# Staging later chunks' k and q in DRAM and loading them by blocks in four transfers

## The chip, the cores and the metric

The kernel runs on one core of a Trainium2 chip. The metric is device time in microseconds (us) from the start to the end of one execution, lower is better; a time given for a kernel is the median of its timed runs. Besides the timed runs there is one profiled execution, from which every duration in this text comes.

## What is computed

An mLSTM cell is followed by a two-layer network with GELU. Shapes: 4 batches (B), 8 heads (H), 768 steps (S), 40 values per head (D); the network takes 3072 tokens of 320 values through 2048 hidden ones and back.

```python
for t in range(S):
    m_new = np.maximum(f_gate[:, :, t] + m, i_gate[:, :, t])
    f_stab = np.exp(f_gate[:, :, t] + m - m_new)
    i_stab = np.exp(i_gate[:, :, t] - m_new)
    C = f_stab * C + i_stab * einsum('bhd,bhe->bhde', vt, kt)
    n = f_stab * n + i_stab * kt
    h_tilde = einsum('bhde,bhe->bhd', C, qt)
    denom = maximum(abs(einsum('bhd,bhd->bh', n, qt)), 1.0)
    y[:, :, t] = sigmoid(o_gate[:, :, t]) * h_tilde / denom
x = y as (tokens, 320)
out = gelu(x @ w_in) @ w_out
```

## The kernel before

**Chunks.** The 768 steps are cut into 6 chunks (c = 0 to 5) of 128 steps. Within a chunk the recurrence is written as matrix products: scores of k against q (`ps`), a weight matrix `W` of exponentials, values (`ph`), what the state of earlier chunks gives (`pf`), and an update of the state. One chunk of all four batches makes 512 tokens (`x`), which then go through the network: `up` (w_in, three products per weight piece, in which x stands as `x_hi`, `x_lo` and `x_all`, and GELU into the tile `g`) and `down` (w_out, in seven half-size products with sums of parts, line L895).

**Order.** The program is traced with a manual schedule: each engine's instructions stand in the order in which they are written. Two strings of words, FRONT and DOWN, are the order by hand. FRONT (the first 129 us) does the gates, the conversion of the weights, chunks 0 and 1 of the cell and chunk 0 of the network. Then, for c = 1 to 5, `up` of chunk c is played, and after it DOWN, which weaves the 14 down products of chunk c (word F) with the cell steps of chunk c+1. The words of DOWN that matter here, by batch number: L3 load batch 3's k and q by blocks (`load_last`), B3 load its row of maxima (`last_M`), K and Q turn k and q (`turn_k`, `turn_q`), C read the state, h update it, V values, M mask, W weights, Y finish, X turn y, R `split_x`, j load batch 0 of the chunk after (`load_next`). K and Q of batches 0 and 1 are done inside `up` (its `turns`).

**Blocks.** For chunks from 2 on, k and q are not transposed by TensorE. They are loaded as 32x32 blocks that VectorE's transpose then turns (L458). `load_blocks` (L153) does this for one batch: for k and q, for the first 32 and the last 8 of the 40 values, and for each of four groups of 32 steps, one transfer from the input: 16 transfers. Batches 0 to 2 go to the tile `blocks`; batch 3 goes into a part of the previous chunk's hidden tile `g` (`load_last`, L443), after GpSimd has zeroed two strips of it (L447, two memsets). The row of maxima of batch 3 also goes into a part of `g` (L177, 512 KB, copied to all partitions), that of the other batches into a tile `W` (L180, 512 KB).

**One queue.** All transfers are issued by SyncE (SP), in order; a transfer whose semaphores are not there yet holds up all behind it. The transfers use eight completion semaphores in turn, so that the n-th waits for the (n-8)-th to have landed. In DOWN the SP order is: batch 3's 16 block transfers, its maxima, then for batches as they are used up k and v (L148, L150) and `W` (L180) for three batches ahead, then 16 block transfers for batch 0 of the next chunk, then o_gate and the outputs.

**Buffers.** `x_lo` and `x_all` are tiles of their own, made once in `products_begin` (L695); `split_x` (L675) writes them for one batch at a time, and the matmuls of `up` (L820, L831) read them.

Of the kernel before, what the change touches and what calls it, by code (L numbers as in the profile page):

```python
# [9 lines left out]
F32 = mybir.dt.float32  # L10
F32R = mybir.dt.float32r
# [5 lines left out]
P = 128  # L17
# [22 lines left out]
def kernel(  # L40
# [16 lines left out]
    nc = tc.nc  # L57

    B, H, S, D = q.shape
    L = P  # L60
    NCH = S // L
# [7 lines left out]
    TG = B * L  # L69
    R = P // 2  # L70
    NX = 2
# [12 lines left out]
    dram = ctx.enter_context(tc.tile_pool(name="dram", bufs=1, space=bass.MemoryType.DRAM))  # L84
# [36 lines left out]
    beyond = gates.tile([P, L], BF16, name="beyond")  # L121
    f_sb = gates.tile([BH, NCH, L], F32, name="f_sb")
    i_sb = gates.tile([BH, NCH, L], F32, name="i_sb")
    M_d = dram.tile([NCH - 1, BH, L], F32, name="M_d")
    swapped_d = [dram.tile([P, n, BH], F32, name=f"swapped{n}") for n in (NCH - 2, NCH - 3)]

# [12 lines left out]
    def load(n, first=0, end=4):  # L139
# [4 lines left out]
        for src, dst in ((q, qb), (k, kb), (v, vb), (o_gate, None))[first:end]:  # L144
            if dst and swapped(c, b):
                x, to = src[b, :, c * L:(c + 1) * L, :].rearrange("h p d -> p h d"), dst[turn_of(n)][:, :, 0:D]
                for i in range(2):
# [2 lines left out]
            nc.sync.dma_start(out=dst[turn_of(n)][:, :, 0:D] if dst else out_of(n),  # L150
                              in_=src[b, :, c * L:(c + 1) * L, :].rearrange("h p d -> p h d"))

    def load_blocks(n, to):  # L153

        c, b = divmod(n, B)
        for i, src in enumerate((k, q)):
            for d, w in ((0, 32), (32, D - 32)):
                for g in range(4):
                    t = c * L + 32 * g
                    nc.sync.dma_start(out=to[64 * i + d:64 * i + d + 32, :, 32 * g:32 * g + w],  # L160
                                      in_=src[b, :, t:t + 32, d:d + w].rearrange("h t d -> t h d"))
# [116 lines left out]
    def decays_last(g0, g1):  # L278
        g = slice(g0, g1)
        pd = ps_tr.tile([P, g1 - g0, BH], F32, name="pd", tag="tr")  # L280
        nc.tensor.matmul(pd.rearrange("p c n -> p (c n)"), last, gT[:, g].rearrange("p c n -> p (c n)"),
                         start=True, stop=True)
        by_half = pd.rearrange("p c (n two) -> p c n two", two=2)
        for hip in range(2):
            nc.vector.tensor_copy(out=dec[halves[hip], g], in_=by_half[halves[hip], :, :, hip])
# [109 lines left out]
    class Cell:  # L395
# [46 lines left out]

        def load_last(self, b):  # L443

            self.by_block = self.before.t[:, 0:HF, 0:P]
            for r in (32, 96):
                nc.gpsimd.memset(self.by_block[r:r + 32], 0.0)  # L447
            load_blocks(self.c * B + b, self.by_block)
# [14 lines left out]
        def turn_q(self, b):  # L463
            self.turn_half(b, 1)
            if b < B - 2:
                load_blocks(self.c * B + b + 1, by_block)
            if self.c < NCH - 1 and b < B - 1:
                self.weigh_values(b)
# [205 lines left out]

        def split_x(self, b):  # L675
            px, t = self.px.pop(b), slice(b * L, (b + 1) * L)
            hi = parts["x"][:, :, t]
            nc.vector.scalar_tensor_tensor(out=parts["x_lo"][:, :, t], in0=px, scalar=-1.0 / BASE, in1=hi, op0=OP.mult, op1=OP.add)
            nc.vector.tensor_tensor(out=parts["x_all"][:, :, t], in0=px, in1=hi, op=OP.subtract)


    HF, HT, HD = NF // 2, TG // 2, DM // 2
# [9 lines left out]
    w_sums, parts, fars, w_hi, w_lo, w_mid = [], {}, [], [], [], {}  # L692
    T = {1: lambda j: w_sums[0][:, j, :], 2: lambda j: w_sums[1][:, j, :], 3: Bm[0][1]}

    def products_begin():  # L695

        gate_ctx.close()
        pool = ctx.enter_context(tc.tile_pool(name="parts", bufs=1))
        w_sums.extend(pool.tile([P, HF, HD], F32, name=f"w_sums{n}") for n in range(2))
        for name in ("x_lo", "x_all"):  # L700
            parts[name] = pool.tile([P, NX + 1, TG], F32R, name=name)
        fars.extend([pool])

    def split_weight():
        i = len(w_lo)
        if i in (0, 3, 5, 8):
            two = shared([P, NX, 2, WP // 2], F32R, "w_in_hi")
            w_hi.extend([two[:, 0], two[:, 1]])
        elif i == 2:
            two = shared([P, 2, 2, WP // 2], F32R, "w_rest_hi")  # L710
            w_hi.append(two[:, 0])
            rest_two.append(two[:, 1])
        elif i == 7:
            w_hi.append(rest_two[0])
        w = w_all[i]
        nc.scalar.activation(out=w_hi[i], in_=w, func=AF.Copy, scale=PART * 2.0 ** -12)
        w_lo.append(w_f(F32R, "w_in_lo"))
        nc.vector.scalar_tensor_tensor(out=w_lo[i], in0=w_hi[i], scalar=-BASE * 2.0 ** 12, in1=w, op0=OP.mult, op1=OP.add)
# [3 lines left out]
    def join_weight(i):  # L722
        w_mid[i] = raw.tile([P, 2, WP // 2], F32R, name="w_in_mid", tag="pow") if i % 5 in (1, 4) else w_f(F32R, "w_mid")
        nc.vector.tensor_tensor(out=w_mid[i], in0=w_hi[i], in1=w_lo[i], op=OP.add)  # L724
# [22 lines left out]
    def hidden_sums(g, f0, f1):  # L747

        (a11, a21), (_, a22) = [[g.t[:, HF * e + f0:HF * e + f1, HT * h:HT * (h + 1)] for h in range(2)]
                                for e in range(2)]  # L750
        s1, s2 = [t[f0 // (HF // 2)][:, f0 % (HF // 2):f0 % (HF // 2) + f1 - f0, :] for t in (g.s1, g.s2)]
        nc.vector.tensor_tensor(out=s1, in0=a21, in1=a22, op=OP.add)  # L752
        nc.vector.tensor_tensor(out=s2, in0=s1, in1=a11, op=OP.subtract)
        nc.vector.tensor_tensor(out=a21, in0=a11, in1=a21, op=OP.subtract)
# [44 lines left out]
    def up(g, sums_too, turns):  # L799

        def split_to(i):
            while len(w_lo) <= i:
                split_weight()

        def pair(f, ahead):

            at = [f // 2 * 5 + f % 2 * 3 + x for x in range(NX)]
            split_to(at[1])
            for i in at:
                if i not in w_mid:  # L810
                    join_weight(i)
            pus = [[pool.tile([P, TG], F32, name="pu", tag=tag) for e in range(2)]
                   for pool, tag in (((ps_h, "h"), (ps_mm, "a")), ((ps_tr, "tr"), (ps_mm, "b")))[f % 2]]
            ahead()
            mid = [w_mid.pop(i) for i in at]
            for n, (w, x) in enumerate((([w_hi[i] for i in at], parts["x"]), ([w_lo[i] for i in at], parts["x_lo"]), (mid, parts["x_all"]))):
                for i in range(2):
                    for e in range(2):
                        for k in range(NX):
                            nc.tensor.matmul(pus[i][e], w[k][:, e, i * P:(i + 1) * P], x[:, k, :],  # L820
                                             start=(n == 0 and k == 0), stop=False, skip_group_check=True)
            return pus

        def rest(u, banks, order):
            mid = w_mid.pop(5 * u + 2)
            for i in order:
                pu = banks[i]
                for n, (w, x) in enumerate(((w_hi[5 * u + 2], parts["x"]), (w_lo[5 * u + 2], parts["x_lo"]), (mid, parts["x_all"]))):
                    for e in range(2):
                        r = halves[e]  # L830
                        nc.tensor.matmul(pu[e], w[r, i // 2, i % 2 * P:(i % 2 + 1) * P], x[r, NX, :], start=False,  # L831
                                         stop=(n == 2), skip_group_check=True)

        def out(i, e, pu):
            nc.scalar.activation(out=g.t[:, HF * e + i, :], in_=pu[e], func=AF.Gelu, scale=4097.0)  # L835

        b0 = pair(0, lambda: split_to(4))
        b1 = pair(1, lambda: join_weight(2))
        for step in turns[:1]:
            step()  # L840
        rest(0, b0 + b1, (0, 1, 2, 3))
        split_to(6)
        join_weight(5)
        join_weight(6)
        for i, pu in enumerate(b0 + b1):
            for e in range(2):
                out(i, e, pu)
        for step in sums_too[:5]:
            step()
        b2 = pair(2, lambda: split_to(9))  # L850
        hidden_sums(g, 0, 2)
        b3 = pair(3, lambda: (hidden_sums(g, 2, 4), join_weight(7)))
        for step in turns[1:] + sums_too[5:]:
            step()
        rest(1, b2 + b3, (2, 3, 0, 1))
        for i, e in ((2, 0), (2, 1), (3, 0), (0, 0), (1, 0), (3, 1), (0, 1), (1, 1)):
            out(4 + i, e, (b2 + b3)[i])
        hidden_sums(g, HF - 2, HF)
        hidden_sums(g, HF - 4, HF - 2)
# [100 lines left out]
    def cell_steps(c, letters, before=None):  # L960
# [11 lines left out]
                 d=lambda: decays_last(0, 1), q=lambda: decays_last(1, NCH - 1), r=halves_out, p=halves_back,  # L972
# [5 lines left out]
    for c in range(1, NCH):  # L978
        g, later, steps = Hidden(True), [], {}
# [38 lines left out]
```

## Time and profile before

| what | value |
|---|---|
| timed runs | 480.09 us median of 3 (479.88 to 480.18) |
| profiled execution | 482.25 us; its span, from the first to the last instruction, 480.3 us |
| busy share of the span | TensorE matmul 98%, weight load 85%, VectorE 73%, ScalarE 46%, GpSimd 16% |
| data queue q1 | 170,368 packets, 43.73 MB, 46.1% of the time of 16 DMA engines |
| instruction queue q8 | 42 packets of 16 KB |
| issues by SP, of these block transfers of L160 | 442, 256 |
| stages | FRONT to 128.7 us; chunk 1: up 128.7 to 157.5, down to 203.8; chunk 2: to 275.5; chunk 3: to 348.2; chunk 4: to 417.8; chunk 5: to the end |

How to read what follows. A timeline row has the start, the duration, the engine, the line, the operation, tiles written and read, the shape and the number of instructions merged; a bracket at its end gives the idle time of the engine before it and what ended that. An fp32 matmul appears as two records, since it is run in two passes. "issue" as a releaser means that the profile shows nothing for which the engine waited. SPq is SP's queue of transfers; its time is that of issuing, not of moving the data. PEclk is the clock that TensorE was granted, 1.00 being full. "DMA share" is the busy share of the core's 16 DMA engines.

### The profile page before, as it was taken

How to read it: one execution, taken by the hardware profiler on the slowest of the kernel's cores; microseconds unless marked ns; L12 is line 12 of the kernel's file. 1: busy time of each engine (PE TensorE's matmuls, PEld its weight loads, DVE VectorE, ACT ScalarE, POOL GpSimd, SP SyncE). 2: the span in 40 equal slices, each digit the busy share in tenths (PEclk: the TensorE clock that was granted, in tenths of full speed). 3: DMA queues.
4: the chain of work that ended last, by engine and by line, in shares of the span. 5: the costliest groups of instructions: out<-in, count | busy, mean ns of one | idle time of the engine just before them, and what ended most of it. 6: DMA issues, size and time to landing. Idle time of an engine off the chain costs nothing.

```text
span 480.3 us, 13250 instructions
## 1 busy us (share of the span) xinstructions
PE 469.6 (98%) x5380; PEld 405.9 (85%) x5380; DVE 353.0 (73%) x774; ACT 222.2 (46%) x477; POOL 74.7 (16%) x104
## 2 busy tenths in 40 slices
PE   8899999999999998999999999999999999999997
PEld 7787888777777997977899977898977899977997
DVE  7899789797879997865599855599865589724321
ACT  6987999844532942104762104862104762112300
POOL 3002200000020324400124400224300115000000
PEclk9999999999999998999999999999999999999999
DMA  9997966279420357541348561258551350100001
GB/s 174 192 224 181 203 159 151 83 196 196 126 30 3 42 103 174 83 97 15 39 74 171 92 123 17 34 91 174 78 122 16 36 88 12 54 2 0 1 1 55
DMA packets 170428, 44.57 MB, mean 93 GB/s; under 512 B 156448, under 2 KB 163904, under 8 KB 170368
## 3 DMA queue, kind: packets, MB, share of 16 engines
q1 hardware_dynamic: 170368, 43.73, 46.1%
q8 instruction: 42, 0.69, 0.6%
q14 instruction: 18, 0.15, 0.1%
HBM read 39.58 MB, written 4.13 MB: 91 GB/s over the span
## 4 chain that ended last, share of the span: by engine, by line
PE 92%; DVE 3%; SPq 1%; DMA 1%; issue 1%; ACT 0%; DVEq 0%
PE po L895 33%; PE pu L820 24%; PE po L872 7%; PE pu L831 6%; PE pu L765 6%; PE ph L625 4%; PE ps L526 2%; PE px L660 2%; PE pu L771 2%; PE pf L581 2%; PE ps L510 1%; SPq L150 1%; PE pf L592 1%; PE pf L548 1%; PE pt L484 1%
## 5 line engine op out<-in xcount | busy, mean ns | idle before, releaser
L895 PE MATMUL po<-w_out,g 128*128 128x160 f32 x640 | 93.7, 305 | 0.0
L895 PEld LDWEIGHTS po<-w_out,g 128*128 128x128 f32 x640 | 89.2, 193 | 2.3 <-ACT g L835 1.8
L835 ACT ACTIVATE g<-pu 128x512 f32<-128x512 f32 x80 | 40.8, 614 | 53.0 <-PE pu L831 52.8
L895 PE MATMUL po<-w_sums,sums 128*128 128x160 f32 x320 | 47.6, 303 | 0.0
L895 PEld LDWEIGHTS po<-w_sums,sums 128*128 128x128 f32 x320 | 44.1, 190 | 0.7
L820 PE MATMUL pu<-x_hi,w_in_hi 128*128 128x512 f32 x160 | 41.7, 403 | 0.0
L820 PE MATMUL pu<-x_lo,w_in_lo 128*128 128x512 f32 x160 | 40.6, 395 | 0.0
L670 ACT ACTIVATE x_hi<-px 128x384 fp32r<-128x384 f32 x20 | 9.8, 489 | 64.3 <-PE px L660 64.3
L435 ACT ACTIVATE W<-W,aT 128x128 f32<-128x128 f32 x128 | 39.2, 389 | 0.1
L820 PEld LDWEIGHTS pu<-x_hi,w_in_hi 128*128 128x128 f32 x160 | 28.5, 188 | 9.4 <-ACT g L835 4.1
L752 DVE TENSOR_TENSOR sums<-g 128x512 f32<-128x512 f32 x20 | 13.7, 687 | 30.8 <-ACT g L835 30.8
L820 PEld LDWEIGHTS pu<-x_lo,w_in_lo 128*128 128x128 f32 x160 | 30.1, 188 | 7.2
L872 PE MATMUL po<-w_out,g 128*128 128x320 f32 x128 | 35.2, 433 | 0.0
L872 PEld LDWEIGHTS po<-w_out,g 128*128 128x128 f32 x128 | 24.0, 190 | 9.6
L835 ACT ACT_TABLE_LOAD x5 | 6.4, 1283 | 55.1 <-DMA blocks<-in_k_dram 27.6
L724 DVE TENSOR_TENSOR w_in_mid<-w_in_hi,w_in_lo 128x512 fp32r<-128x512 f32 x20 | 13.8, 689 | 24.4 <-PE pu L820 24.4
L820 PE MATMUL pu<-x_all,w_mid 128*128 128x512 f32 x80 | 31.6, 395 | 0.0
L820 PE MATMUL pu<-x_all,w_in_mid 128*128 128x512 f32 x80 | 31.6, 395 | 0.0
L447 POOL MEMSET g<- 32x1024 f32 x8 | 7.6, 945 | 147.9 <-ACT W L435 122.4
L409 POOL TENSOR_SCALAR_AFFINE_SELECT W<-W 128x1024 f32<-128x1024 f32 (+2 forms) x20 | 20.9, 1057 | 55.0 <-DMA W<-M_d 54.7
L765 PE MATMUL pu<-first_x,w_in 128*128 128x256 f32 x128 | 29.1, 382 | 0.0
L908 DVE TENSOR_TENSOR o_sb<-po,o_sb 128x320 f32<-128x320 f32 (+1 forms) x27 | 12.5, 461 | 20.7 <-PE po L895 16.7
(183 smaller groups left out, 909.5 us busy)
## 6 DMA issues: line engine op xcount, KB each, us to landing
W<-M_d SPq DMA_DIRECT2D x16, 512.0 KB, 5.1
bits<-in_moe_w_in_dram SPq DMA_DIRECT2D x20, 256.0 KB, 4.4
bits<-in_moe_w_out_dram SPq DMA_DIRECT2D x16, 320.0 KB, 3.2
ob<-in_o_gate_dram SPq DMA_DIRECT2D x24, 160.0 KB, 3.5
out_dram<-o_sb SPq DMA_DIRECT2D x24, 160.0 KB, 2.3
vb<-in_v_dram SPq DMA_DIRECT2D x14, 160.0 KB, 5.0
kb<-in_k_dram SPq DMA_DIRECT2D x14, 160.0 KB, 4.9
g<-M_d SPq DMA_DIRECT2D x4, 512.0 KB
```

The lines of the kernel that those rows point to most:

```text
L409: nc.gpsimd.affine_select(out=x, in_=x, compare_op=OP.is_ge, fill=1.0e30, base=base, pattern=[[0, H], [1, x.shape[2]]], channel_multiplier=-1)
L435: nc.scalar.activation(out=W[n][:, h, :], in_=src, func=AF.Exp, scale=-1.0, bias=aT[:, self.c, r:r + 1])
L625: nc.tensor.matmul(ph[r, h, :], Pm[:, h, r], vb[turn_of(n)][:, h, :], start=True, stop=True)
L724: nc.vector.tensor_tensor(out=w_mid[i], in0=w_hi[i], in1=w_lo[i], op=OP.add)
L752: nc.vector.tensor_tensor(out=s1, in0=a21, in1=a22, op=OP.add)
L765: nc.tensor.matmul(banks[-1][e][:, i - i0, :], in_tile(i, x)[:, e, i % 2 * P:(i % 2 + 1) * P], first_x[:, x, t0:t1], start=(x == 0 and i = ...
L820: nc.tensor.matmul(pus[i][e], w[k][:, e, i * P:(i + 1) * P], x[:, k, :], start=(n == 0 and k == 0), stop=False, skip_group_check=True)
L831: nc.tensor.matmul(pu[e], w[r, i // 2, i % 2 * P:(i % 2 + 1) * P], x[r, NX, :], start=False, stop=(n == 2), skip_group_check=True)
L835: nc.scalar.activation(out=g.t[:, HF * e + i, :], in_=pu[e], func=AF.Gelu, scale=4097.0)
L872: nc.tensor.matmul(po[b], g.t[:, f, b * L:(b + 1) * L], w_out[:, f, :], start=(f == 0), stop=(f == NF - 1))
L895: nc.tensor.matmul(bank[at][:, i, :], lhs(j, t), rhs(j), start=(first and i == 0 and j == 0), stop=(i == n - 1 and j == HF - 1), skip_grou ...
L908: nc.vector.tensor_tensor(out=to, in0=pb, in1=x, op=OP.add)
```

## The change

The k and q of chunks 2 to 5 are first copied within DRAM, to one piece per chunk and batch in which the rows of all heads follow each other (`kq_d`). From batch 2 of chunk 2 on, `load_blocks` then reads this copy: since heads and groups of steps are one dimension there, four transfers per batch (two for k, two for q) take the place of 16. Batches 0 and 1 of chunk 2 are loaded as before. The copies are issued by SP: chunk 2's batches 2 and 3 (4 copies) as the first thing of `up` of chunk 1, and a later chunk's (8 copies of 160 KB) in `up` of the chunk two before it, after batch 1's K and Q. Batch 3's blocks no longer go into `g`, but into the memory of `x_lo`: both are tiles of one tag with one buffer, so that `load_last` takes the buffer when `up` is done with `x_lo`, and `split_x` of batch 0 takes it back. The strings FRONT and DOWN stay as they are.

```diff
+    kq_d = [[dram.tile([B, H * L, D], F32, name=f"{x}{c}_d") for x in "kq"] for c in range(2, NCH)]
...
+    def copy_chunk(c):
+
+        for b in range(B) if c > 2 else range(2, B):
+            for to, src in zip(kq_d[c - 2], (k, q)):
+                for x, y in ((src[b, :, c * L:(c + 1) * L, :], to[b]),):
+                    nc.sync.dma_start(out=y.rearrange("(h x t) d -> x h (t d)", h=H, x=16),
+                                        in_=x.rearrange("h (x t) d -> x h (t d)", x=16))
+
     def load_blocks(n, to):
...
             for d, w in ((0, 32), (32, D - 32)):
+                if n > 2 * B + 1:
+                    nc.sync.dma_start(out=to[64 * i + d:64 * i + d + 32].rearrange("t h (g w) -> t (h g) w", w=32)[:, :, 0:w],
+                                      in_=kq_d[c - 2][i][b, :, d:d + w].rearrange("(x t) d -> t x d", t=32))
+                    continue
                 for g in range(4):
...
         def load_last(self, b):
-            self.by_block = self.before.t[:, 0:HF, 0:P]
+            self.by_block = fars[0].tile([P, H, P], F32, name="blocks3", tag="x_lo", bufs=1)
...
         def split_x(self, b):
+            if b == 0:
+                parts["x_lo"] = fars[0].tile([P, NX + 1, TG], F32R, name="x_lo", tag="x_lo", bufs=1)
...
     def products_begin():
-        for name in ("x_lo", "x_all"):
-            parts[name] = pool.tile([P, NX + 1, TG], F32R, name=name)
+        parts["x_all"] = pool.tile([P, NX + 1, TG], F32R, name="x_all")
...
     def up(g, sums_too, turns):
+        if c == 1:
+            copy_chunk(2)
         b0 = pair(0, lambda: split_to(4))
...
         for step in turns[1:] + sums_too[5:]:
             step()
+        if c + 2 < NCH:
+            copy_chunk(c + 2)
         rest(1, b2 + b3, (2, 3, 0, 1))
```

## The prediction

> **What bounds the kernel now.** I read the page's busy shares first, then TensorE's waits, then the stage where they fall, then SP's timeline there. The page:
>
> ```profile
> PE 469.6 (98%) x5380; PEld 405.9 (85%) x5380; DVE 353.0 (73%) x774; ACT 222.2 (46%) x477; POOL 74.7 (16%) x104
> PEclk9999999999999998999999999999999999999999
> q8 instruction: 42, 0.69, 0.6%
> ```
>
> TensorE is the bound, so the change can win only what TensorE idles, and it touches nothing before 128.7 us. Its matmul waits from 157 us on, and the same place in the timeline and in the table of stretches (columns: stretch, length, busy time of PE, PEld, DVE, ACT, POOL, clock, DMA share, GB/s):
>
> ```profile
> PE ph L625 <- issue: 3.0, 4, 1.8
> ```
>
> ```profile
> 183.25 0.81 PE L592 MATMUL pf<-vw,kb 128*40 128x41 f32 x32
> 183.99 0.42 PE L625 MATMUL ph<-vb,W 128*32 128x41 f32 x23
> 186.25 0.59 PE L625 MATMUL ph<-vb,W 128*32 128x41 f32 x41 [1.84 <-issue]
> 186.77 4.12 PE L895 MATMUL po<-w_out,g 128*128 128x160 f32 x16
> ```
>
> ```profile
> 157.50:183.50 26.00, 26.00 (x558) 24.75 (x558) 25.30 (x60) 17.40 (x45) 10.17 (x11) 1.00 0.55 96
> 183.50:191.00 7.50, 5.66 (x128) 5.14 (x125) 5.30 (x16) 0.65 (x3) 2.25 (x4) 0.77 0.51 119
> ```
>
> TensorE stops four times (1.84, 0.24, 0.26 and 0.63 us, at 186.3, 262.5, 318.3 and 335.7), each time inside a row of `ph` matmuls, where nothing is waited for. Counted in TensorE's records, the stops stand at 3,991, 6,018, 7,289 and 8,049: distances of 8 x 253.4, 5 x 254.2 and 3 x 253.3. The queue named "instruction" moved 42 packets of 16 KB for 10,760 records, 256 each. So I read the stops as waits for the next piece of TensorE's own program. The packet records agree: pieces landed at 184.63, 261.11, 316.67 and 334.02, and TensorE went on 1.62, 1.38, 1.58 and 1.69 later. After the long stop the clock was halved from 187.32 to 190.73, and 16 L895 matmuls took 4.12 where 16 of the same take 2.44 elsewhere (259.65): 1.68 more. The change can win 2.97 + 1.68 = **4.65 us** of the profiled span here.
>
> The Trainium skill ("Runtime: NRT & Kernel Launch", Instruction fetch mechanics) says that crossing such a 16 KiB boundary is mostly hidden; by it these stops would be something else and the change would give 480.1. The distances speak against it.
>
> **Why the fetch is late.** SP before the long stop:
>
> ```profile
> 155.10 3.76 SPq L160 DMA_DIRECT2D blocks<-in_k_dram  x8
> 158.96 3.85 SPq L160 DMA_DIRECT2D blocks<-in_q_dram  x8
> 163.96 4.69 SPq L160 DMA_DIRECT2D g<-in_k_dram  x8
> 168.69 5.82 SPq L160 DMA_DIRECT2D g<-in_q_dram  x8
> 174.61 0.40 SPq L177 DMA_DIRECT2D g<-M_d  x1
> 175.11 1.31 SPq L148 DMA_DIRECT2D kb<-in_k_dram  x2
> ...
> 177.89 0.56 SPq L180 DMA_DIRECT2D W<-M_d  x1
> ...
> 179.66 2.46 SPq L180 DMA_DIRECT2D W<-M_d  x1
> ```
>
> Sixteen issues of 0.45 us and their delays hold SP until 174.5. Then three 512 KB loads and the k and v loads go out together, and the packet records show all 16 engines full from 176 to 184. When a piece is asked for is not shown; I put it 48 records before TensorE reaches the piece ahead of it, because the five fetches of chunk 4, without traffic, then all start 1.0 to 1.3 us after that. From request to use, a fetch then takes 3.66 with no traffic (401.29 to 403.38, and the mean 1.57); 4.62 (313.63 to 318.25) beside small packets; 5.02 and 5.14 (257.47 to 262.49, 330.57 to 335.71) in full traffic, and 6.94 (179.31 to 186.25) at the long stop. What it may take, where it is tight: 4.9, 4.2 and 5.1 in chunk 1 (needed at 167.8, 171.4, 184.4), 5.1 and 4.8 in chunk 2 (244.0, 262.2), 5.0, 4.4, 5.0, 4.5 in chunk 3 (314.2, 318.0, 331.1, 335.1). Chunk 4's are looser or without traffic.
>
> The skill ("DMA: Bandwidth & Descriptors", Queues, rings and completion order) says that an engine changes between queues packet by packet, so that a backlog of data should hold a fetch for one packet only; by that emptying the queue earlier wins nothing, 480.1 again. The 1.4 us and more between no and full traffic are against it.
>
> **The change, part by part.**
> - Issues removed: 14 loads x 12 = 168, at 0.45 (the median of L160): 76 us of SP time, none on TensorE's path. The packets stay the same, 32 and 128 bytes; a load of 1,024 packets issues in 0.42 to 0.53 (L150 kb), so four take 2 us.
> - Issues added: 28 copies. No copy within DRAM is in the trace. Issue: 0.40 (outputs, 160 KB) to 0.70 each, I take 0.5; eight take 3.2 to 5.6, I take 4. Landing: 2.3 (outputs) to 4.0 (M_d<-M). Engine time: 128 packets of 1,280 bytes at 55 ns (outputs) each, 3.5 us per eight copies, 7 if reading and writing add up. Hidden: the first batch 2 load that needs them comes over 20 us later in chunk 1 (132.8 to 155.1); the other copies have a whole chunk.
> - Batch 3's blocks in `x_lo`: the memsets (2 x 0.97) wait for the last L831 (157.3, 232.5) and no longer for L754 (163.8, 237.8), so they, and the GpSimd work queued behind them, start no later. `split_x` must now wait for VectorE's own transposes (177.8 against 194.1), 16 us of cover; without it x, and with it `up`, would be late by the same amount.
> - The SP order after it, chunk 2: batch 2 228.7 to 230.6, copies to 235 (239 at the upper bounds), batch 3 to 237 (241), maxima at 238 to 241 (before: 248.3), k and v when `ph` of batch 0 frees them at 243.5 (248.8), the W loads at 245.5 and 247.5 (251.8, 253.6). So the burst ends near 253 in place of 260, and in chunk 1 near 178 in place of 184. The compute that uses the maxima (mask, weights of batch 3) moves ahead too; TensorE does not wait for it now, so that is worth nothing.
> - Waits of ScalarE fall away, and are worth nothing. The two rows below have the same 13.8 in other chunks where TensorE is named, and the table load at 216.19 starts when L831 has finished its first bank:
>
> ```profile
> ACT L835 <- DMA blocks<-in_k_dram: 27.6, 2, 13.8
> ACT L835 <- PE pu L831: 27.5, 2, 13.8
> ```
>
> - Fetches after it: those needed at 184.4, 262.2 and 331.1 run after the burst and become free. Those at 167.8, 171.4, 244.0, 314.2 and 318.0 now meet copies, maxima or k and v that came later before. At 171.4 and 318.0, the tightest, I take 4.88, between 4.62 and 5.14, and at 335.1 4.62: 0.7 + 0.5 + 0.1 = **1.3 us** of stops. With 3.66 everywhere it is 0; with 5.14 everywhere 0.24 + 0.94 + 0.04 + 0.04 + 0.34 + 0.14 + 0.74 + 0.14 + 0.64 = 3.3. A stop of 0.63 cost no clock, one of 1.84 did.
>
> **Sum.** Profiled: 4.65 - 1.3 = 3.35 off 482.25. The timed median is 2.16 under the profiled execution (its span, 480.3, and 1.95 around it). If that much of the stops is the profiler's own, timed runs have only 2.49 of them and win 1.2; if none is, 3.35. The middle, 2.3, gives **477.8 us**.
>
> **Rivals.**
> 1. *The fetch's delay does not follow the queue, or the copies fill the gap they make* (the change does not do what it should): as many stops as before, **480.1**. For it: beside small blocks a fetch still takes 4.62. Against: the three longest are in the burst.
> 2. *The burst moves onto the tightest fetches* (171.4, 318.0): k and v now come exactly when these are asked for, where before only small blocks did, and it happens again in what remains at 335.1. If a fetch takes 6.0 there, towards the 6.94 seen, the two stop 1.8 and 1.6, each long enough for the clock's 1.68: 6.8, less the 4.65 (or 2.49) won: +2.1 to +4.3, **482.2 to 484.4**. It decides from about 5.5 per fetch on, where stops of 1.3 and 1.1 and one loss of clock (4.1) eat the win.
> 3. *All stops go*: 4.65 less, **475.4**.
>
> **How the numbers follow.** Forecast (a win of 1.0 to 4.0 us) 0.51; rival 3 0.09; rival 1 0.20, rival 2 0.20. Faster by over 0.2% (1 us, about what a measurement of this kernel can tell) 0.60, within 0.2% 0.20, slower 0.20. The range for 8 in 10 leaves out half of rival 2 and little below: 475.5 to 482.0; the forecast's own range is 476.1 to 479.1.
>
> **What would show it.** Right: the bracket of 1.84 and the 4.12 row gone, PEclk 1.00 there, g<-M_d issued 7 to 10 us earlier after `up`, TensorE's "issue" near 1.3. Wrong: stops with 253 records between them that stay or grow near 171 and 318; a K or Q transpose (L458) that waits for its blocks; SP held by copies past 241.

## The result and the profile after

The changed kernel takes **478.53 us** (median of 20 runs, 477.38 to 480.93), the kernel before 480.58 in the same set of runs (20 runs): a ratio of 0.9959, 95% interval 0.9945 to 0.9974, 2.05 us less. In a second set it was 479.67 against 481.46, 0.9966 (0.9944 to 0.9988). The forecast was 477.8, with 475.5 to 482.0 as its range. The profiled execution went from 482.25 to 479.66, its span from 480.3 to 477.7. Sets of runs are not on the same chip, and the median of the kernel before moves from 480.58 to 481.46 between them, so kernels are compared below by their ratio to the kernel before of their own set. The ratio on record is worked out from all runs of a set and is not exactly the quotient of the two medians (for the longer program below it is 0.9893, the medians give 0.9909).

The page of the changed kernel:

```profile
PE 467.2 (98%) x5380; PEld 404.4 (85%) x5380; DVE 348.8 (73%) x774; ACT 221.7 (46%) x477; POOL 70.3 (15%) x104
PEclk9999999999999999999999999999999999999999
q8 instruction: 42, 0.69, 0.6%
```

TensorE does the same work (x5380, 42 pieces of program), and the clock's dent is gone from this profile: it is at full speed from 6.0 to 477.0 us. TensorE's waits after 125 us, then the new stop and, behind it, the place of the old one in the timeline, and the two stretches of the prediction:

```profile
PE ph L638 <- issue: 2.3, 2, 1.7
```

```profile
171.14 0.78 PE L638 MATMUL ph<-vb,W 128*32 128x41 f32 x58
173.63 0.28 PE L638 MATMUL ph<-vb,W 128*32 128x41 f32 x6 [1.71 <-issue]
...
186.24 0.81 PE L638 MATMUL ph<-vb,W 128*32 128x41 f32 x64
186.98 2.44 PE L913 MATMUL po<-w_out,g 128*128 128x160 f32 x16
```

```profile
157.50:183.50 26.00, 24.29 (x480) 22.84 (x477) 24.63 (x62) 18.33 (x47) 8.23 (x10) 1.00 0.77 159
183.50:191.00 7.50, 7.50 (x255) 6.95 (x254) 5.99 (x19) 0.32 (x1) 2.66 (x5) 1.00 0.36 61
```

Four stops have become two. Those at 186, 262 and 336 are gone: all 64 `ph` matmuls near 186 run in one row, and the 16 matmuls behind them take 2.44 where they took 4.12. But the `ph` row at 171.14 breaks off after 58 and TensorE stands for 1.71, where the row of the kernel before runs through:

```profile
170.75 0.90 PE L625 MATMUL ph<-vb,W 128*32 128x41 f32 x64
```

And the stop of 0.26 at 318.3 has grown to 0.63, at 316.7. In chunk 1 the loss has moved from the second stretch into the first. SP there:

```profile
157.91 0.83 SPq L159 DMA_DIRECT2D k_d<-in_k_dram  x1
158.78 0.60 SPq L159 DMA_DIRECT2D q_d<-in_q_dram  x1
...
163.33 1.15 SPq L168 DMA_DIRECT2D blocks<-k_d  x2
164.52 2.76 SPq L168 DMA_DIRECT2D blocks<-q_d  x2
167.46 0.43 SPq L190 DMA_DIRECT2D g<-M_d  x1
167.98 1.36 SPq L149 DMA_DIRECT2D kb<-in_k_dram  x2
...
174.45 1.63 SPq L193 DMA_DIRECT2D W<-M_d  x1
```

The maxima (`g<-M_d`) now leave at 167.46 (before: 174.61), in chunk 2 at 239.07 (248.30), in chunk 3 at 310.93 (319.16), and the k, v and `W` loads follow at once. From 180 to 184, where the DMA share was 1.18, it is 0.03.

By chunk (from the first L834 matmul of one `up` to that of the next) the lengths went from 75.06, 71.56, 72.69 and 69.62 to 73.23, 71.11, 71.95 and 69.71, 2.93 less in all; FRONT ends 0.37 later.

### The profile page after: what moved, and what is told of

Same layout as the page of the kernel before. It is cut to its first block, busy times and chain, and to the rows that moved or that the text cites. A ratio compares the mean times of both kernels' runs of the same rounds, so it can differ in the third digit from the quotient of the medians.

```text
span 477.7 us, 13017 instructions
## 1 busy us (share of the span) xinstructions
PE 467.2 (98%) x5380; PEld 404.4 (85%) x5380; DVE 348.8 (73%) x774; ACT 221.7 (46%) x477; POOL 70.3 (15%) x104
## 4 chain that ended last, share of the span: by engine, by line
PE 92%; DVE 3%; SPq 1%; DMA 1%; issue 1%; ACT 0%; DVEq 0%
PE po L913 33%; PE pu L834 24%; PE po L890 7%; PE pu L845 6%; PE pu L779 6%; PE ph L638 4%; PE ps L539 3%; PE px L673 2%; PE pu L785 2%; PE pf L594 2%; PE ps L523 1%; SPq L151 1%; PE pf L605 1%; PE pf L561 1%; PE pt L497 1%
## 5 line engine op out<-in xcount | busy, mean ns | idle before, releaser
L913 PE MATMUL po<-w_out,g 128*128 128x160 f32 x640 | 92.1, 301 | 0.0
L913 PEld LDWEIGHTS po<-w_out,g 128*128 128x128 f32 x640 | 87.6, 190 | 2.3 <-ACT g L849 1.9
L913 PE MATMUL po<-w_sums,sums 128*128 128x160 f32 x320 | 47.7, 303 | 0.0
L913 PEld LDWEIGHTS po<-w_sums,sums 128*128 128x128 f32 x320 | 44.1, 190 | 0.7
L834 PE MATMUL pu<-x_hi,w_in_hi 128*128 128x512 f32 x160 | 41.8, 403 | 0.0
L834 PE MATMUL pu<-x_lo,w_in_lo 128*128 128x512 f32 x160 | 40.5, 395 | 0.0
L834 PEld LDWEIGHTS pu<-x_hi,w_in_hi 128*128 128x128 f32 x160 | 28.5, 188 | 9.4 <-ACT g L849 4.1
L834 PEld LDWEIGHTS pu<-x_lo,w_in_lo 128*128 128x128 f32 x160 | 30.0, 188 | 7.2
L890 PEld LDWEIGHTS po<-w_out,g 128*128 128x128 f32 x128 | 24.0, 190 | 9.6
L834 PE MATMUL pu<-x_all,w_mid 128*128 128x512 f32 x80 | 31.6, 395 | 0.0
L834 PE MATMUL pu<-x_all,w_in_mid 128*128 128x512 f32 x80 | 31.6, 395 | 0.0
L779 PEld LDWEIGHTS pu<-first_x,w_in 128*128 128x128 f32 x128 | 23.8, 190 | 3.3 <-DVE w_in L390 0.2
```

The costliest lines, as they stand in the source:

```text
L779: nc.tensor.matmul(banks[-1][e][:, i - i0, :], in_tile(i, x)[:, e, i % 2 * P:(i % 2 + 1) * P], first_x[:, x, t0:t1], start=(x == 0 and i = ...
L890: nc.tensor.matmul(po[b], g.t[:, f, b * L:(b + 1) * L], w_out[:, f, :], start=(f == 0), stop=(f == NF - 1))
L913: nc.tensor.matmul(bank[at][:, i, :], lhs(j, t), rhs(j), start=(first and i == 0 and j == 0), stop=(i == n - 1 and j == HF - 1), skip_grou ...
```

## The experiments

**Theory:** a piece of TensorE's program is late when its request meets the burst of loads; the change moves the burst. **Rivals:** A, only the buffer counts, since batch 3's blocks need not wait for `g`; B, the copies and their larger packets; C, fewer waits on VectorE and ScalarE; and that the stops belong to the work, not to the program's pieces. "Grid" means the places at which the pieces begin.

**x_lo alone.** The kernel before with

```diff
-            self.by_block = self.before.t[:, 0:HF, 0:P]
+            self.by_block = fars[0].tile([P, H, P], F32, name="blocks3", tag="x_lo", bufs=1)
```

and the tile `x_lo` made in `split_x`, as in the change.

> The kernel before with one part of the change: batch 3's blocks go to x_lo's buffer, still in sixteen pieces per load and with no copies. Theory (the gain is time of SP: the burst of loads moves away from the late pieces of TensorE's program): sixteen pieces still take 7.6 us, but in chunk 1 they need not wait for L754 (163.9), so g<-M_d comes at about 170.5 in place of 174.6, in chunk 2 at about 246 in place of 248.3: a part of the gain, -0.5 to -1.3 us against the kernel before. Rival A (it is the freed buffer that wins, not the count of issues): the whole gain, -1.8 to -2.5. Rival B (the copies and the larger elements win) and rival C (fewer semaphore waits on VectorE and ScalarE win): within 0.3 us of the kernel before.

Measured: 479.38 against 481.11, **0.9953** (0.9935 to 0.9970). Within the intervals that is the whole gain (the changed kernel ran in other sets), as rival A had it; my figure for the theory was too small. Stops of 1.36 at 185.7 and 0.24 at 260.3 are left, and no clock is lost. What I left out is chunk 3. SP there, in this kernel:

```profile
305.90 4.48 SPq L160 DMA_DIRECT2D blocks<-in_k_dram  x8
310.42 4.84 SPq L160 DMA_DIRECT2D blocks<-in_q_dram  x8
315.43 0.39 SPq L177 DMA_DIRECT2D g<-M_d  x1
```

Before, the first of these waited for `g` till 309.44, and the maxima came at 319.16. By 3.7 us sooner is enough: the pieces used near 329 and 332 start 1.47 and 1.26 after I take them to be asked for (before: 2.36 and 2.52), and both stops of chunk 3's end are gone.

**Batch 3 back in g.** The changed kernel with the old `load_last`, and

```diff
-                if n > 2 * B + 1:
+                if n > 2 * B + 1 and n % B < B - 1:
```

> The changed kernel with batch 3's blocks back in g, in sixteen pieces from the inputs (its copies are made and not read); batches 0 to 2 keep copies and four transfers. Theory: SP needs 10.5 us for the g pieces after the copies, so g<-M_d is back at about 174.5 and 248.5 and the stops near 186 and 262 return: within 0.5 us of the kernel before, the fetch after the long stop halving the clock again. Rival A: the same. Rival B (copies and packets) and rival C (fewer semaphore waits): two thirds or more of the gain stay, -1.3 to -2.1.

Measured: 480.92 against 481.11, **0.9989** (0.9968 to 1.0010), as the theory and A expected. The copies are made, ten of the 14 loads still read them, and VectorE's trace has 203 semaphore instructions where the kernel before has 263 and the changed one 179, and yet nothing is won: B is out, and so is C for VectorE. ScalarE's 12 instructions of that kind, which the change also removes, come back here with `g` (75 before, 75 here, 63 with the change), so that this run does not part them from A; but no stop of TensorE in these three profiles is put down to ScalarE. `g<-M_d` leaves at 175.56, 246.86 and 317.43, and four stops are there: 0.78 at 186.2, 0.24 at 261.2, 0.93 at 330.5 and 0.36 at 334.6, three of them where the kernel before has one. The clock was not halved in the profiled run, in which the longest stop is 0.93.

**Copies that nobody reads.** As the last, with `if False:` in place of the condition, so that sixteen pieces are issued behind the copies.

> The kernel before, with the change's copies added at their places and read by nobody: sixteen pieces per load, batch 3's in g. Theory: the copies cost SP 5.2 us ahead of batch 3's pieces, g<-M_d comes at about 179 and 253 in place of 174.6 and 248.3, the burst ends later; stops as many as before or more, 0 to +2.5 us against the kernel before. Rival B (what wins is what the copies do to the traffic): -1 to -2. Rivals A and C: within 0.3 us of the kernel before.

Measured: 493.93, **1.025** (1.0215 to 1.0284), 12.8 us slower; the theory had 0 to 2.5.

```profile
PE ps L539 <- DVE qT L471: 6.4, 5, 2.4
PEclk9999999999999999999998999998999999999999
```

With 5.2 us of copies ahead of 10 us of pieces, batch 3's blocks come too late for their own reader: TensorE waits for `qT`, and twice the clock falls. So the four transfers are what makes room for the copies. This is a limit that I had not seen; two late pieces of program (0.85 and 0.71) stand beside it, and the 12.8 us were not taken apart further.

**A longer program.** The changed kernel with TensorE's first matmuls replaced (they only warm it up):

```diff
-    warm(6)
+    short(30)
...
+    def short(n):
+        cold = ps_h.tile([P, P], F32, name="cold", tag="h")
+        for _ in range(n):
+            nc.tensor.matmul(cold[0:32, 0:16], w_out[:, 0, 0:32], w_out[:, 0, 0:16], start=True, stop=True, skip_group_check=True)
```

> The changed kernel with TensorE's program 96 records longer ahead of its first real work: the six 128 x 128 matmuls that warm it up are replaced by thirty of 32 x 16 (four records each), nothing else. Theory (a stop stands every 253 records where the piece is late): every stop is found 96 records earlier in the work. Near 173.6 and 316.7 no stop is left; stops can only stand near 188, 240, 244, 330, 382 and 400, each of 0.2 to 0.4 us if a piece takes 4.7 us from request to use: about 1.1 us in all after chunk 0 where it was 2.3, so -1.2 us, less 0 to 3 us for the thirty matmuls if they take longer than the six did (read the lengths of chunks 1 to 3, which leave that out). Rival (the stops belong to places in the work, not to the grid of the program): stops at 173.6 and 316.7 of the same length, no change.

Measured: 476.72 against 481.11, **0.9893** (0.9863 to 0.9922). No stop above 0.12 us is left after chunk 0, and FRONT ends when it did (129.08). The stretch from 172 to 176, first in the changed kernel, then in this one:

```profile
172.00:176.00 4.00, 2.37 (x22) 2.31 (x23) 3.19 (x8) 1.18 (x5) 2.80 (x4) 1.00 0.90 196
```

```profile
172.00:176.00 4.00, 4.00 (x30) 4.00 (x31) 3.85 (x9) 1.14 (x4) 2.50 (x3) 1.00 1.14 221
```

The traffic is as dense (1.14 against 0.90) and the work the same; TensorE is busy for all 4 us: the piece that is fetched there is needed only at 179.1. So traffic with no piece due stops nothing, and neither does the work.

**The kernel before, longer program.** The same edit.

> The kernel before with TensorE's program 96 records longer at its start (thirty 32 x 16 matmuls for the six 128 x 128), nothing of the change. Theory 1 (two things set the stops together: where the 253-record grid falls, and when the loads burst; the change moves only the second): stops move 96 records earlier, to near 241, 245, 257, 332, 384 and 402, 0.5 to 1.0 us in all instead of 2.97, and no loss of clock: 478 to 479, 1.5 to 2.5 us under the kernel before, and the change is then worth 1 to 2 us more at this grid (476.7 was measured with it). Theory 2 (the change pays only where the grid happens to fall badly): the same 476.7 within 0.5 as the changed kernel at this grid. Theory 3 (the gain of the longer program comes from something else in the changed kernel): no change against before.

Measured: 480.52 against 481.19, **0.9982** (0.9958 to 1.0007). Both theories' figures missed, and theory 3's fits better: at this grid the kernel before loses about as much as at its own. The stops did move, to 183.8, 257.2 and 328.1 (0.68, 0.51 and 0.52, in `ph` and `pf`), three where the two profiles of the kernel before have four and three, and of the six places that theory 1 had named only the one near 257 is among them; with them came a wait for ScalarE's `g` (0.57):

```profile
PE pf L597 <- issue: 0.7, 1, 0.7
PE ph L630 <- ACT g L440: 0.6, 1, 0.6
```

**x_lo alone, longer program.** The same edit again.

> Batch 3's blocks in x_lo's buffer, sixteen pieces, no copies, and TensorE's program 96 records longer at its start. Theory 1: the burst stands where it stood with x_lo alone (174, 246, 315), pieces needed near 183, 257 and 332 fall into its end: 0.4 to 0.8 us of stops, 477 to 478. Theory 2: 476.7, as with the whole change. If the copies and the four transfers are what wins, this lies over 1 us above 476.7.

Measured: 479.48, **0.9953** (0.9934 to 0.9972), over theory 1's 477 to 478. Stops of 0.38 at 184.3 and 0.56 at 328.9 in the burst's end, and a wait of 0.40 for VectorE behind the first. Here the copies and the four transfers on top of x_lo are worth 2.8 us (479.48 against 476.72, whose own sets' medians of before differ by 0.08), or about 2 by the second measurement of that kernel, below; at the grid of the change as it stands no gain from them shows.

**A bad place of the grid.** The changed kernel with `short(50)`: 176 records more.

> The changed kernel with TensorE's program 176 records longer at its start (fifty 32 x 16 matmuls for the six): a place of the grid chosen to be bad. Theory 1: the time from the request of a piece to its use is at its shortest near 185 (2.3 us), 327 (2.8), 259 (4.2), 168 and 311 (4.5). Both worst places now lie in quiet traffic, where a piece takes 3.7: stops of 1.4 and 0.9 and small ones of 0.3 to 0.5 in sum, 2.6 to 5.3 in all against the 2.33 of the changed kernel, with or without 1.7 us of clock each: 479 to 483. If the fetch has no fixed price even in quiet traffic, or the grid is not what sets the stops: 478.5 as the changed kernel.

Measured: 482.61 against 481.19, **1.0032** (1.0011 to 1.0053): with the whole change in it, slower than the kernel before. Of this, FRONT ends 1.46 later (the fifty take 5.5, the six 2.9). Stops of 0.76 and 0.72 stand where they were expected (185 and 327, with the delays ahead of them at 187.7 and 332.1), shorter than the 1.4 and 0.9 that I had; one of 1.06 at 246.7, in traffic, I had not. The first two come without traffic: their packets start 1.07 and 1.45 after my request times, but the work between request and use lasts only 2.3 and 2.8 us. So a burst is one way for a piece to be late, and too little work ahead of it is another.

**Copies early.** `copy_chunk(c + 2)` goes from its place after `turns[1:]` to one ahead of the first `rest`.

> The changed kernel with each chunk's copies issued about 15 us earlier, ahead of the first rest of up, where the queues are idle; same copies, same loads. Theory 1: SP saves 5.2 us behind the blocks of batch 2, so batch 3's blocks and g<-M_d leave at 158 to 162, 230 to 234 and 302 to 305, and only k, v and W are left near 171 and 316 (k and v wait for ph of batch 0 in chunks 2 and 3): the stop at 173.6 falls from 1.71 to 0.5 to 1.2, the one at 316.7 to 0.3 to 0.6, so -0.5 to -1.3 us against the changed kernel. Rival (k, v and W themselves hold the piece, wherever the copies and M_d are): both stops as they were, no change.

Measured: 479.42 against 481.19, **0.9961** (0.9944 to 0.9977), as the changed kernel. The stops did what the theory said, and more: 0.12 at 171.7, none at 316. A wait took their place:

```profile
PE po L913 <- ACT o_sb L936: 1.6, 3, 0.6
```

Against the stop-free run, TensorE loses 0.83, 0.68 and 0.78 there, once per chunk. In the compiled program the first L913 matmul of this group waits for ScalarE's count, where that of the changed kernel waits for VectorE's; why the place of the copies moves that wait I did not find out.

**Second profiles, and traffic alone.** The changed kernel and its longer program again, the latter with one more copy per chunk, behind `g<-M_d`:

```diff
         def last_M(self, b):
             load_M(self.c * B + b, self.before.t[:, 0:HF, P:2 * P])
+            if self.c > 0:
+                nc.sync.dma_start(out=extra_d[self.c - 1].rearrange("(h x) y -> x h y", h=H),
+                                  in_=q[0, :, 0:4 * L, :].rearrange("h (x t) d -> x h (t d)", x=16))
```

> The changed kernel once more, unaltered, for a second profile and for times beside the next two. If its stops belong to the program and the traffic, they stand at the same two places (near 172 and 316) and measure 1.5 to 2.5 us in all; if a stop's length is a matter of chance from one execution to the next, they differ by more than 0.5 us each. Time 478 to 479.

> The changed kernel with TensorE's program 96 records longer at its start, once more, on the same chip as the changed kernel: 1.5 to 2.3 us under it if the first measurement (476.7) was the grid, no stop above 0.3 us after chunk 0. If that first measurement was luck, within 0.8 us of the changed kernel.

> The same program for TensorE as the changed kernel with 96 more records, with traffic alone added: right after g<-M_d one more copy within DRAM of 655 KB (eight heads of four chunks of q, read by nobody), one issue per chunk. Theory (the queue's traffic makes the pieces of the program late): stops come back where the copy's packets meet a request: 0.5 to 2 us near 244 (no slack left there), 0.3 to 1.5 near 171, 0 to 0.5 near 314; 1 to 4 us in all, perhaps with waits of TensorE for vb or W, which now stand behind the copy, and these would be seen by their names. Rival (the stops are set by SP or by semaphores, not by traffic): no stops, within 0.5 us of the kernel without the copy.

> The kernel before once more, one look, for a second profile: its stops near 186, 262, 318 and 336 at the same records as in the first; 2.5 to 3.5 us in all if they belong to program and traffic. The halved clock after the first of them is expected only if that stop is again 1.8 us or longer.

Measured, all against 481.46: the changed kernel 479.67 (0.9966); with the longer program **477.36** (0.9915, 0.9894 to 0.9937), again no stop; with the copy 479.17 (0.9962, 0.9939 to 0.9984), 1.8 slower than without it. With the copy there is one stop in the profiled run, and it is where the theory had it; the row without the copy first:

```profile
243.11 4.73 PE L918 MATMUL po<-w_out,g 128*128 128x160 f32 x32
```

```profile
243.39 0.95 PE L922 MATMUL po<-w_out,g 128*128 128x160 f32 x5
246.39 4.79 PE L922 MATMUL po<-w_out,g 128*128 128x160 f32 x21 [2.05 <-issue]
```

The instruction packets there start at 244.02 with the copy and at 241.61 without, while TensorE was only 0.28 later. TensorE's program is the same and SP's other issues keep their order, so it is the added traffic that makes the piece late. Near 171 and 314, where the theory had stops too, none came.

The second profiles: the changed kernel stops 0.42, 0.79 and 0.35 (at 168.6, 173.2, 316.1), the kernel before 1.48, 0.23 and 0.23 (at 186.4, 317.1, 333.9), with no clock lost. So most places repeat (the stop of 0.24 at 262 is missing, the one at 168.6 is new), and a stop's length varies by up to 0.9; the 1.94 in all of the kernel before is less than I had expected. By chunk this pair is 73.25, 71.95, 72.01 and 69.63 against 72.95, 71.12, 71.89 and 69.63: 1.25 less in all, which is also what the first pair's 2.93 leaves without the 1.68 of the clock.

**The grid.** Fourteen profiles were taken, and eleven have stops on "issue" of over 0.2 us after chunk 0. Counted in TensorE's records, all of these stand at 3,231, 3,485, 3,991 to 3,995, 4,245 to 4,247, 5,515, 6,018 to 6,021, 7,289, 7,795 to 7,799 or 8,049 to 8,051: 3,991 plus a multiple of 253.6, within 4, whether the program has 0, 96 or 176 records more at its start. In the work the stops move; in the program they don't.

## Why the prediction was right, and where it was off

The forecast's cause held, and its time was 0.7 us low; 0.5 of that is the kernel before itself (480.58 in this set, 480.09 when the forecast was made), for the win was 2.05 where 2.3 was forecast. That these two are so near is partly luck, as the steps show:

- **The stops are late pieces of TensorE's own program, behind the burst.** Shown from both sides: by the grid (longer program, no stop) and by traffic alone (one more copy, one stop of 2.05).
- **The pieces needed at 184.4, 262.2 and 331.1 become free.** They did: their packets start 0.91, 1.04 and 1.01 after my request times, in place of 3.94, 2.72 and 2.36.
- **SP.** `g<-M_d` at 238 to 241 in chunk 2: 239.07. 7 to 10 us earlier: 7.2, 9.2 and 8.2. A copy costs 0.60, not 0.5, eight of them 5.2, not 4, inside the bounds. GpSimd, `split_x` and the transposes (L471) made TensorE wait nowhere.
- **ScalarE's waits for blocks are worth nothing.** Right. In the changed kernel the DMA is gone from them, and the same time is put down to TensorE (before: 27.6 and 27.5):

```profile
ACT L849 <- PE pu L845: 55.2, 4, 13.8
```

- **The term that was mis-sized: "At 171.4 and 318.0, the tightest, I take 4.88".** At 318 it took 4.99 and 4.73 in the two profiles. At 171.4 it took 5.97 and 5.72, with packets that start 3.46 after the request (before: 1.46): rival 2's 6.0. I had k and v falling on that piece, but the maxima, 512 KB, go out right ahead of them. So 2.33 us of stops were left (1.56 in the second profile) where I had 1.3. Rival 2 is right at one of its two places. Its other half, that such a stop also costs the clock, did not happen at 1.71, and this was luck of the stop's place (last section).
- **The sum.** Profiled: stops 2.97 to 2.33 and the clock's 1.68 to nothing, 2.32 of the 2.59 measured; forecast 3.35. A stop costs some 0.2 more than it stands: held against the stop-free run, stops of 1.48, 0.79 and 0.35 cost 1.67, 1.00 and 0.56. With two stops fewer that makes 0.4 more; FRONT ended 0.37 later here and 0.06 earlier in the second pair, so that is scatter.
- **"The timed median is 2.16 under the profiled execution".** I split this between profiler and stops. It is mostly the clock: the kernel before has a mean clock of 0.996 or less in 8 of 35 timed runs of one set and in 5 of 21 of another, and the median of those is some 2 us higher; the median run has no such loss, and the first profiled one had. Nor did the change remove that loss: 6 of 30 timed runs of the changed kernel have it, and 17 of 79 of the kernel before, in the three sets for which its clocks are on record. So the 1.68 is no part of what the median won; among the runs of the second set without the loss the medians are 479.26 and 481.26, still 2.00 apart. Of the 2.05 the chunks of the profiles, without the clock, show 1.25. The rest is not settled: a stop's length varies by as much, and the interval of the ratio is 1.2 to 2.6 us.
- **What I had not weighed: which part of the change is needed.** I costed the x_lo buffer by its waits alone, and put the gain on 168 issues. On this grid the buffer alone wins as much (0.9953 against 0.9959). Copies and four transfers move the burst 4 to 7 us further, off some pieces and onto others, and no gain on balance shows. With 96 records more they gain 2 to 3.

What stays open: when a piece is asked for (48 records ahead is only consistent with the packets), what the rest of the timed gain is, and a program that has both the early copies and the longer start, which was not tried. Of all versions the changed kernel with the longer program is the fastest: 476.72 and 477.36.

## What to carry to other kernels

When the busiest engine stands in the middle of a row of equal instructions and nothing is named as the cause, count the records between such stops: equal distances point to the fetch of its program, and a few dozen dummy instructions at the start move all of them, for better or worse. Judge a change in the order of loads at more than one such offset before crediting it: here the same edit was worth 2 us at one and 3 to 4 at another, and at a third the changed kernel was slower than the old one at its own (the old one was not run at the third). A change of many parts should be taken apart: here the smallest part, one buffer, gave as much as the whole at the offset at which the change was judged.

## What the runs showed of the hardware

- Without traffic a piece of TensorE's program mostly starts to arrive 0.9 to 1.6 us after my request time (0.91, 1.04 and 1.01 in the changed kernel). In full traffic, where a stop of over 0.4 followed, it was 2.2 to 4.7 us; but full traffic does not always delay it (1.38 for the piece needed at 312.0 in the changed kernel's second profile). The Trainium skill ("Runtime: NRT & Kernel Launch", Instruction fetch mechanics) has the crossing mostly hidden; here it is hidden only where the work of some 300 records before it lasts longer than the fetch, and stops of up to 2.05 us stand where it does not.
- The clock is halved for 3.41 us after a stop of 1.84 and of 2.05, after a wait of 2.36 for data, and after two of 1.54 and 0.31 close together; stops of 1.71 and 1.48 and a wait of 1.91 leave it alone. What parts them is the place. In every profile that records the clock, its changes inside the span lie whole multiples of 3.413 us apart (53 in the kernel before, 138 in the changed one). Cut into such windows, the four in which TensorE idles for 1.73 to 2.36 us are each followed by one at half clock, and no other window up to 470 us idles for more than 1.42 or is followed by half clock. The wait of 1.91 lay across two windows (1.24 and 0.67), and of the stop of 1.71 only 1.31 lay in one. The Trainium skill ("TensorE: Matmul & The Clock Gate", Why this matters for your kernels) advises against gaps of more than about 3 us; here 1.84 was enough, and the measurement decides.
- A copy within DRAM of 160 KB takes 0.60 us of SP's time and lands after 3.2 to 3.4.
